# Products of probabilities and v for two query blocks in one session, one copy for both

## The chip, the cores and the metric

The kernel runs on one core of a Trainium2 chip. A core has TensorE (PE; its weight loads are listed as PEld), VectorE (DVE), ScalarE (ACT), GpSimd (POOL), SyncE (SP) and 16 DMA engines. The metric is the device time of one execution in microseconds. Lower is better.

## The reference

One transformer block over 2048 tokens of width 640. The condition `c` gives six modulation rows. The first half is sliding-window attention with 32 heads of 20 dimensions, in which a query sees itself and the 255 keys before it. The second half is an MLP of width 1536.

```python
mod = (_silu(c) @ w_mod).reshape(c.shape[0], 6, 1, -1)
h = _layernorm(x, axis=-1) * (1 + ca) + sa
# _A_ref: qkv = h @ wqkv; scores = q k^T * 20 ** -0.5
mask = (idx[:, None] - idx[None, :] >= 0) & (idx[:, None] - idx[None, :] < 256)
p = _softmax(jnp.where(mask, scores, -1e9), axis=-1)
x = x + ga * ((p @ v) @ wo)
h = _layernorm(x, axis=-1) * (1 + cb) + sb
x = x + gb * (_gelu(_layernorm(h) @ w1 + b1) @ w2 + b2)
```

## The kernel before, in words

Values that need more than one pass are split into a high and a low part, and each product is three matmuls (high x high, high x low, low x high). The program has four stretches: a prologue (first projections of q and k, modulation columns, the layer norm of the first tokens), the attention's loop, the passage to the second half, and the MLP. Every instruction goes through a helper that keeps the program's order on each engine, so the profile shows nearly all of them under line 193 (L193) and they are told apart by their tiles.

**The loop.** Its iterations are numbered `t`. The tokens are split into two halves of 1024 (`half`), the heads into 8 groups of four (`quad`), and a half into 8 query blocks of 128 (`qb`); 2 x 8 x 8 = 128 items. In iteration `t` there are, in this order:

- Scores `s` of item `t` (query by key), for the row maxima alone, and scores `e` of item `t - 11` (key by query; `LAG = 11`), for the exponentials. `score_batch` issues both as one batch of matmuls of 60 or 62 rows.
- `e_mask`: DVE masks `e`.
- `pv_stage`: a session of products of probabilities `pt` and `vbuf` (or `vcar`, the two key blocks carried from the first half). It runs in columns of 32, four heads beside each other, into PSUM tile `o`. A query block needs up to three key blocks, so a session has 4, 8 or 12 matmuls, which the profile shows as 8, 16 or 24 instructions, since each runs in two passes.
- `pv_copy`: ScalarE copies `o` to half of the tile `oT`. In the iterations of `SUMS_LAST` this stands behind the exponentials, otherwise ahead of them.
- `e_exp`: ScalarE takes the exponential of `e` into `pt` (five buffers, `NPT`), and GpSimd cuts the two triangles by two selections.
- `s_max`: DVE masks `s` and takes the maxima `nm`, in two pieces, or in one in the iterations of `WHOLE`.
- Four quarters `h` = 0 to 3, with whatever a plan has put there: at 0 and 2 the projection products (`pp`) of later heads, at 1 small turns that go through the `o` bank (`take_aside`), elsewhere loads, splits and casts, and from iteration 115 on the first work of the second half (`wo`, `xt`, `yt`).
- `pv_store`: a DMA from ScalarE's queue stores `oT`, once per two query blocks.

A query block's session stands in iteration `LAG + PVLAG + 8 * (8 * half + quad) + qb + half`, with `PVLAG = 2`: two iterations after the newest `pt` it reads was made.

**The planner.** `lay_units` spreads the 810 products of 54 projection units over the iterations up to `LAST = 108`. It finds by bisection a `room` per iteration, subtracts what turns cost, and adds the corrections of `EXTRA`. `UNITS` is the units' order, `EARLY` says when weights are split, `AFTER` delays turns. `LOV` lists units whose low parts DVE makes (GpSimd the rest), `HIA` casts that ScalarE makes. `MODS`, `WOS`, `W1S`, `RS`, `LNS`, `LATE_AT`, `TAIL0`, `NEXT`, `TAIL_AT`, `SHIFTS` and `MOVE` are times and engines of other pieces. `prepare` splits the MLP's weights in 18 pieces: ScalarE casts the high part, the engine of `PREPE` ("p" GpSimd, "d" DVE) subtracts for the low part, at the times of `PREP`. `WARM` puts idle matmuls into the loop, `ORDER` is the prologue's order.

Of the kernel before, what the change touches and what calls it, by code (L numbers as in the profile page):

```python
# [17 lines left out]
P = 128  # L18
# [9 lines left out]
VW = 21  # L28
# [4 lines left out]
PVLAG = 2  # L33
# [4 lines left out]
ORDER = 'T00 S0 L00 M1 R5 S1 R7 S2 T01 R3 S3 L01 N R6 P00 R6 M2 R2 T02 M3 P01 T03 L02 T10 R1 L10 L03 R5 C P02 T11 M4 T04 P10 T13 T12 L04 L12 L11 L13 P03 P04 E0 T14 L14 P11 Y00 P12 P13 Y01 P14'  # L38
LOWP = ['L00', 'L03', 'L10', 'L12', 'L04', 'L14', 'L02', 'L13']


UNITS = ((0, 'q1', 'k1', 'v0', 'v1', 'k2', 'q2', 'v2', 'q3', 'k3', 'v30', 'k40', 'q40', 'v40', 'q41', 'k41', 'v31', 'v41'), (1, 'q10', 'k00', 'q00', 'k10', 'q01', 'k01', 'k11', 'q11', 'v0', 'v1', 'k2', 'q2', 'k3', 'q3', 'v2', 'q4', 'v3', 'k4', 'v4'))
FAST = 10
LNS = [-10.75, -3.75, -1.0, -1.5, 1.75, -0.5, -0.25]
LOV = [1, 8, 15, 17, 18, 24, 25, 28, 31, 35, 37, 43, 44, 47, 52, 54, 55, 57]
HIA = [2, 5, 7, 9]
# [22 lines left out]
WOS = [86.25, 92.25, 98.25, 108.5, 111.75, 113.25, 118.0]
W1S = [126.25, 123.5]  # L70
RS = [[79.75, 80.25], [82.25, 84.25]]
# [4 lines left out]
NEXT = [133.869, 138.782]  # L76
# [3 lines left out]
TAIL_AT = {'rd': -1.3068, 'ri': -0.9678, 'load': -0.9467, 'om': -0.2491, 'oh': 0.0039, 'ol': 0.1278, 'w00': 0.2982, 'w01': 0.3513, 'w02': 0.405, 'w03': 0.4739, 'w04': 0.5616, 'add0': 0.569, 'sa0': 0.8046, 'w10': 0.711, 'w11': 0.7249, 'w12': 0.7775, 'w13': 0.7979, 'w14': 0.8778, 'add1': 0.885, 'sa1': 1.1777, 'm0': 1.3428, 'x0': 1.368, 'x1': 1.5837, 'm1': 1.344, 'sb0': 1.5278, 'sb1': 1.5966, 'n2': 1.7395, 'y0': 1.8473, 'y0l': 1.9709, 'y1': 2.026, 'y1l': 2.1439, 'xs': 1.5892}  # L80
# [9 lines left out]
PREPO = ['a0', 'a1', 'a2', 'a3', 'a4', 'a5', 'b0', 'b1', 'b2', 'b3', 'b4', 'b5', 'b6', 'b7', 'b8', 'b9', 'b10', 'b11']  # L90
PREP = [8.5, 14.5, 16.0, 24.0, 26.75, 29.0, 38.0, 39.75, 42.75, 49.75, 52.0, 53.75, 63.5, 66.25, 67.25, 74.5, 77.75, 79.75]
PREPS = [0.75, 1.25, 1.75, 1.25, 1.5, 0.5, 1.25, 1.75, 2.0, 1.0, 2.0, 2.5, 1.5, 2.5, 1.25, 1.25, 2.5, 1.75]
PREPE = 'pppppppddpppppppdp'
SHIFTS = {'xs.3': 0.0692, 'sb1.3': 0.0208, 'n2.3': 0.082, 'y0.3': 0.0208, 'y0l.3': 0.1499, 'y1.3': 0.229, 'y1l.3': 0.1312, 'y1.1': 0.0411, 'add0.3': 0.0437, 'sb0.4': -0.2255, 'n2.4': -0.3097, 'rd.1': -0.0806, 'w13.3': 0.0057, 'm1.4': -0.0777, 'x0.4': -0.0148, 'sb1.4': -0.2131, 'x1.4': -0.0788, 'w03.0': -0.0911, 'w13.0': 0.0783, 'xs.0': 0.0616, 'sa0.3': -0.1054, 'y1l.2': -0.0153, 'add1.3': 0.0891, 'x0.3': -0.1271, 'x1.0': -0.0318, 'sb1.0': -0.0318, 'rd.4': 0.0708, 'w04.0': -0.1766, 'add0.0': -0.1766, 'oh.2': -0.1264, 'ol.2': -0.1264, 'sa0.4': 0.1411, 'load.0': 0.0158, 'm0.3': -0.1391, 'x0.2': -0.0056, 'sb0.2': -0.0056, 'w13.1': -0.0028, 'sb0.3': -0.0998, 'x1.3': -0.0998, 'oh.3': 0.0453, 'ol.3': 0.0453, 'y1l.1': -0.0306, 'w10.2': -0.0083, 'w11.2': -0.0083, 'w12.2': -0.0083, 'ri.4': 0.0976, 'w10.3': -0.0663, 'ol.0': -0.0707, 'xs.2': 0.0752, 'w10.4': 0.0088, 'w10.0': -0.0992, 'sa0.1': -0.0354, 'w14.1': -0.0354, 'add1.1': 0.1001, 'y0l.1': 0.0457, 'sa1.1': -0.0249, 'w10.1': -0.0656, 'sa0.0': 0.0999, 'y0.4': -0.1354, 'xs.4': -0.1354, 'y0l.4': -0.1354, 'y1.4': -0.1354, 'y1l.4': -0.1354, 'n2.1': -0.0627, 'n2.2': 0.0408, 'y0.2': 0.0408, 'y0l.2': 0.0408, 'y1.2': 0.0408, 'x1.2': -0.0924, 'm0.0': -0.0138, 'w00.1': 0.0058, 'w01.1': 0.0058, 'w02.1': 0.0058, 'rd.3': -0.1006, 'w03.4': -0.0047, 'w02.0': -0.0393}
ROWS = [0, 1, 0, 0, 2, 0, 0, 0, 6, 0, 1, 5, 2, 0, 0, 1]
AHEAD = 5.25
# [102 lines left out]
def block_kernel(ctx: ExitStack, tc: tile.TileContext, x, wqkv, wo, w1, b1, w2, b2, c, crow, wmod, wcol, sel, outT):  # L199
# [1667 lines left out]
```

## Time and profile before

| | us |
|---|---|
| median of three runs | 961.62 (961.39 to 962.18) |
| profiled execution | 960.75 |
| its span | 959.0 |

| engine | busy, us | share of the span |
|---|---|---|
| PE | 932.4 | 97% |
| PEld | 739.9 | 77% |
| DVE | 657.8 | 69% |
| POOL | 498.7 | 52% |
| ACT | 412.0 | 43% |

The attention's loop fills about 50 to 580 us of the span; sessions run from 106.5 to 578.8. A timeline row gives start, length, engine, line, operation, output and inputs, the shape and how many instructions were merged into it; what stands in brackets is idle time ahead of it and what ended it. PE's lengths overlap, since its instructions are pipelined; distances between starts are what counts. "PEclk" is the clock granted to TensorE, as a share of full speed.

### The profile page before, as it was taken

How to read it: one execution, taken by the hardware profiler on the slowest of the kernel's cores; microseconds unless marked ns; L12 is line 12 of the kernel's file. 1: busy time of each engine (PE TensorE's matmuls, PEld its weight loads, DVE VectorE, ACT ScalarE, POOL GpSimd, SP SyncE). 2: the span in 40 equal slices, each digit the busy share in tenths (PEclk: the TensorE clock that was granted, in tenths of full speed). 3: DMA queues.
4: the chain of work that ended last, by engine and by line, in shares of the span. 5: the costliest groups of instructions: out<-in, count | busy, mean ns of one | idle time of the engine just before them, and what ended most of it. 6: DMA issues, size and time to landing. Idle time of an engine off the chain costs nothing.

```text
span 959.0 us, 20088 instructions
## 1 busy us (share of the span) xinstructions
PE 932.4 (97%) x7685; PEld 739.9 (77%) x7685; DVE 657.8 (69%) x1104; ACT 412.0 (43%) x729; POOL 498.7 (52%) x671
## 2 busy tenths in 40 slices
PE   9999999999999999999998899999999999999998
PEld 8867677776777777777676678888888888888886
DVE  5564878889768787766879977795557667633332
ACT  3633555576755565555544553441221324311111
POOL 3533656787966555375455556886242655311020
PEclk8999999999999999999989999999999999999999
DMA  8356989879799877945763439564649957644285
GB/s 311 99 191 184 343 260 327 279 214 303 243 310 282 275 228 253 289 144 144 222 183 103 127 99 337 152 223 143 241 166 332 300 178 242 214 167 177 104 278 188
DMA packets 109183, 212.34 MB, mean 221 GB/s; under 512 B 9856, under 2 KB 43104, under 8 KB 107552
## 3 DMA queue, kind: packets, MB, share of 16 engines
q1 hardware_dynamic: 99872, 202.67, 65.1%
q10 hardware_dynamic: 9216, 8.39, 2.8%
q8 instruction: 61, 1.00, 0.4%
q14 instruction: 34, 0.28, 0.1%
HBM read 137.44 MB, written 72.81 MB: 219 GB/s over the span
## 4 chain that ended last, share of the span: by engine, by line
PE 81%; DVE 10%; ACT 3%; DMA 2%; issue 2%; SPq 1%; POOL 0%; DVEq 0%; ACTq 0%; POOLq 0%
PE pp L193 17%; PE out L193 16%; PE P L193 15%; PE o L193 7%; PE e L193 7%; PE wo L193 6%; PE s L193 4%; DVE nm L193 2%; ACT pt L193 2%; DVE e L193 2%; PE ppo L193 2%; DVE s L193 1%; PE warm L193 1%; PE psx L193 1%; DMA wc<-in_wcol 1%
## 5 line engine op out<-in xcount | busy, mean ns | idle before, releaser
L193 POOL TENSOR_SCALAR_AFFINE_SELECT pt<-pt 128x512 f32<-128x512 f32 x192 | 131.8, 687 | 127.6 <-ACT pt L193 120.6
L193 PE MATMUL out<-ghi,w 128*128 128x512 f32 x480 | 168.3, 395 | 0.0
L193 ACT ACTIVATE pt<-e 128x1024 f32<-128x1024 f32 (+1 forms) x120 | 133.7, 1115 | 64.0 <-DVE e L193 61.1
L193 DVE TENSOR_REDUCE nm<-s 128x1 f32<-128x256 f32 (+4 forms) x194 | 156.7, 836 | 4.4
L193 PE MATMUL e<-qbuf,kbuf 62*128 62x128 f32 (+2 forms) x773 | 113.4, 330 | 13.2 <-ACT pt L193 11.7
L193 PEld LDWEIGHTS e<-qbuf,kbuf 62*128 62x128 f32 x773 | 80.8, 186 | 52.9 <-ACT pt L193 30.2
L193 PE MATMUL pp<-hhi,w_hi 128*128 128x512 f32 x265 | 114.8, 433 | 0.3
L193 PE MATMUL s<-kbuf,qbuf 60*128 60x384 f32 (+2 forms) x728 | 107.2, 305 | 3.4 <-DVE stage L193 1.4
L193 PE MATMUL pp<-hlo,w_hi 128*128 128x512 f32 x265 | 108.1, 408 | 0.0
L193 DVE COPY_PREDICATED e<-mask_t,e 128x512 f32<-128x512 uint32 x96 | 66.5, 693 | 58.3 <-PE e L193 51.4
L193 PE MATMUL pp<-hhi,w_lo 128*128 128x512 f32 x265 | 105.8, 399 | 0.0
L193 PEld LDWEIGHTS out<-ghi,w 128*128 128x128 f32 x480 | 90.1, 188 | 17.4 <-issue 0.7
L193 PE MATMUL o<-pt,vbuf 128*32 128x128 f32 x2688 | 100.6, 279 | 0.0
L193 PEld LDWEIGHTS s<-kbuf,qbuf 60*128 60x128 f32 x728 | 88.0, 187 | 13.9 <-DVE nm L193 5.5
L193 PE MATMUL out<-glo,w 128*128 128x512 f32 x240 | 93.9, 391 | 0.0
L193 POOL TENSOR_TENSOR w_lo<-wraw,w_hi 128x128 fp32r<-128x128 f32 x171 | 76.3, 478 | 23.7 <-ACT w_hi L193 21.9
L193 PE MATMUL P<-yhi,w1s 128*128 128x512 f32 x264 | 88.2, 389 | 0.0
L193 DVE COPY_PREDICATED s<-mask_t,s 128x512 f32<-128x512 uint32 x112 | 77.1, 688 | 14.7 <-PE s L193 14.7
L193 ACT COPY oT<-o 128x128 f32<-128x128 f32 x128 | 33.8, 264 | 119.0 <-PE o L193 116.8
L193 PEld LDWEIGHTS o<-pt,vbuf 128*32 128x32 f32 x2688 | 67.5, 110 | 15.3 <-issue 2.5
L193 PEld LDWEIGHTS pp<-hhi,w_hi 128*128 128x128 f32 x265 | 49.8, 188 | 22.1 <-issue 10.0
L193 PE MATMUL wo<-wo_h,ot_hi 128*128 128x320 f32 x256 | 60.9, 321 | 0.1
(230 smaller groups left out, 1782.0 us busy)
## 6 DMA issues: line engine op xcount, KB each, us to landing
w<-w_scr SPq DMA_DIRECT2D x48, 640.0 KB
qbuf<-q_scr SPq DMA_DIRECT2D x60, 240.0 KB
wraw<-in_wqkv SPq DMA_DIRECT2D x36, 320.0 KB
w_scr<-prep SPq DMA_DIRECT2D x18, 640.0 KB
kbuf<-k_scr SPq DMA_DIRECT2D x44, 240.0 KB
q_scr<-stage SPq DMA_DIRECT2D x20, 512.0 KB
k_scr<-stage SPq DMA_DIRECT2D x20, 512.0 KB
ws_scr<-w1s SPq DMA_DIRECT2D x6, 1536.0 KB
```

The source lines that it names most:

```text
L193: return self.tc.keep_in_program_order(op(*args, **kw))
```

## The change

A session makes two query blocks (`b` for blocks 2b and 2b + 1) one after the other, into the two halves of one `o` tile of 128 x 256, and one ScalarE copy empties it. There are 64 sessions in place of 128, with the same matmuls in all. A pair's session stands one iteration after its newest `pt` was made (`PVLAG = 1`); of the four pairs of a quad they fall on the item numbers 1, 3, 5 and 6 (+ `half`), plus `LAG + 1`. `pv_at` is made ahead of the planner, which charges each such iteration `PV_COST` products. A new table `SPOT` moves some sessions, with their copy, from behind the batch to a quarter of the iteration. The loop's tables are new.

```diff
-PVLAG = 2
+PVLAG = 1
-WARM = {(114, 3): 2, (135, 0): 1}
-LATE_AT = [105.25, 106.5, 107.25, 108.5, 110.75, 111, 113.5]
+WARM = {}
+LATE_AT = [105.75, 106.0, 106.75, 108.5, 109.75, 110.75, 114.25]
-PREP = [8.5, 14.5, 16.0, 24.0, 26.75, 29.0, 38.0, 39.75, 42.75, 49.75, 52.0, 53.75, 63.5, 66.25, 67.25, 74.5, 77.75, 79.75]
-PREPE = 'pppppppddpppppppdp'
+PREP = [7.5, 14.0, 15.0, 22.5, 25.5, 27.0, 36.75, 38.75, 41.75, 48.75, 50.0, 54.75, 63.5, 66.5, 67.5, 74.0, 79.0, 80.5]
+PREPE = 'ppppdpddpdddddddpd'
+PV_COST = 1.9833
+SPOT = {99: 3, 40: 3, 44: 3, 128: 2, 115: 1, 118: 1, 69: 1, 54: 1, 119: 3, 107: 3, 11: 3, 45: 3, 51: 3, 14: 2, 123: 3, 111: 3, 89: 3, 76: 3, 29: 1, 12: 3, 134: 3, 77: 2, 68: 2, 36: 3, 116: 1, 136: 1, 129: 3, 55: 2, 103: 2, 91: 2, 100: 3, 135: 2, 97: 3, 81: 1, 60: 1, 59: 1, 38: 1, 84: 3, 80: 3, 32: 2, 126: 1, 20: 1}
...
-    def pv_stage(half, quad, qb):
+    def pv_stage(half, quad, b):
         q = quads[half, quad]
-        ob = pools["o"].tile([P, P], F32, tag="o", name=f"o{half}_{quad}_{qb}")
...
+        ob = pools["o"].tile([P, 2, P], F32, tag="o", name=f"o{half}_{quad}_{b}")
+        for c in range(2):
+            qb = 2 * b + c
+            kbs = [kb for kb in range(qb - 2, qb + 1) if (kb, qb) in q["p"]]
+            for kb in kbs:
+                v = vblk(half, quad, kb)
+                pt, col = q["p"][kb, qb]
+                for i, h in enumerate(HEADS):
+                    matmul(
+                        ob[32 * h : 32 * h + 32, c], v[:, h * VW : h * VW + 32], pt[:, i, col : col + P],
+                        start=kb == kbs[0], stop=kb == kbs[-1], tile_position=(0, 32 * h), skip_group_check=True,
+                    )
...
-        nc.scalar.copy(q["oT"][:, c], ob)
+        q["oT"] = att.tile([P, 2, P], F32, tag="oT", bufs=2, name=f"oT{half}_{quad}_{b}")
+        nc.scalar.copy(q["oT"], ob)
...
+                u = min(2 * b + 1, 6) + half
+                pv_at.setdefault(LAG + PVLAG + (half * QUADS + quad) * NQB + u, []).append((half, quad, b))
...
+        for t in pv_at:
+            used[t] += PV_COST
...
-        sums = [(*key, pv_stage(*key)) for key in pv_at.get(t, ())]
+        sums = [] if t in SPOT else [(*key, pv_stage(*key)) for key in pv_at.get(t, ())]
...
+            if SPOT.get(t) == h:
+                for key in pv_at.get(t, ()):
+                    pv_copy(*key, pv_stage(*key))
```

Also new, with other numbers in the same form: `ORDER` (35 warming matmuls in both), `LOWP`, `UNITS`, `LNS`, `LOV`, `HIA`, `EXTRA`, `EARLY`, `AFTER`, `SUMS_LAST`, `WHOLE` (51 iterations of the main part before, 36 now), `MODS`, `WOS`, `W1S`, `RS`, `NEXT`, `TAIL_AT`, seven entries of `MOVE`, `PREPS`, `SHIFTS`, `ROWS` and `AHEAD`.

More of the change, by code (lines that the diff above doesn't have):

```diff
@@ new lines @@
+AFTER = {0: 2, 2: 3, 4: 4, 5: 2, 6: 1, 7: 1, 8: 2, 9: 1, 10: 2, 11: 2, 12: 1, 14: 2, 15: 1, 19: 1, 20: 1, 21: 2, 22: 1, 23: 2, 27: 1, 32: 1, 34: 1, 35: 1, 36: 2, 38: 3, 39: 6, 40: 2, 41: 1, 47: 4, 48: 1, 45: 4, 42: 2, 51: 3, 59: 1, 60: 2, 17: 2, 18: 1, 54: 1, 46: 1, 43: 1, 44: 1}
+SUMS_LAST = [15, 19, 26, 29, 33, 35, 42, 43, 50, 63, 65, 71, 74, 76, 79, 83, 86, 87, 88, 89, 90, 92, 93, 103, 104, 105, 106, 107, 108, 110, 111, 113, 114, 116, 117, 118, 119, 120, 121, 126, 130, 131, 133, 135, 136, 139, 140]
@@ L70 @@
-W1S = [126.25, 123.5]
-RS = [[79.75, 80.25], [82.25, 84.25]]
+MODS = [[7.25, 16.0], [18.0, 27.0], [68.75, 80.0], [54.75, 65.0]]
+WOS = [90.25, 93.5, 101.25, 109.25, 113.25, 114.25, 117.0]
+W1S = [124.5, 122.75]
+RS = [[79.5, 80.75], [88.75, 91.0]]
 TOMID = 109
-WARM = {(114, 3): 2, (135, 0): 1}
-LATE_AT = [105.25, 106.5, 107.25, 108.5, 110.75, 111, 113.5]
+WARM = {}
+LATE_AT = [105.75, 106.0, 106.75, 108.5, 109.75, 110.75, 114.25]
 TAIL0 = [115.25, 120.25, 124.25, 129.25]
-NEXT = [133.869, 138.782]
+NEXT = [133.869, 138.574]
@@ L97 @@
+ROWS = [2, 1, 0, 0, 4, 0, 0, 0, 2, 0, 0, 5, 4, 0, 0, 4]
+AHEAD = 4.75
 W2B = 3
@@ L774, in e_exp, with pv_copy, pv_store @@
             )
-    def pv_stage(half, quad, qb):
+    def pv_stage(half, quad, b):
         q = quads[half, quad]
-        ob = pools["o"].tile([P, P], F32, tag="o", name=f"o{half}_{quad}_{qb}")
-        kbs = [kb for kb in range(qb - 2, qb + 1) if (kb, qb) in q["p"]]
-        for kb in kbs:
-            v = vblk(half, quad, kb)
-            pt, col = q["p"][kb, qb]
-            for i, h in enumerate(HEADS):
-                matmul(
-                    ob[32 * h : 32 * h + 32], v[:, h * VW : h * VW + 32], pt[:, i, col : col + P],
-                    start=kb == kbs[0], stop=kb == kbs[-1], tile_position=(0, 32 * h), skip_group_check=True,
-                )
+        ob = pools["o"].tile([P, 2, P], F32, tag="o", name=f"o{half}_{quad}_{b}")
[10 more added lines that the diff above has]
+                    )
         return ob
-    def pv_copy(half, quad, qb, ob):
+    def pv_copy(half, quad, b, ob):
         q = quads[half, quad]
-        b, c = divmod(qb, 2)
-        if c == 0:
-            q["oT"] = att.tile([P, 2, P], F32, tag="oT", bufs=2, name=f"oT{half}_{quad}_{b}")
-        nc.scalar.copy(q["oT"][:, c], ob)
-        if qb == NQB - 1:
-            done_v.add(half * QUADS + quad)
-    def pv_store(half, quad, qb):
-        b, c = divmod(qb, 2)
-        if c:
-            t0 = half * HALF + b * 256
-            nc.scalar.dma_start(o_scr[quad * 4 : quad * 4 + 4, :, t0 : t0 + 256], quads[half, quad]["oT"].rearrange("p c t -> p (c t)"))
+        q["oT"] = att.tile([P, 2, P], F32, tag="oT", bufs=2, name=f"oT{half}_{quad}_{b}")
+        nc.scalar.copy(q["oT"], ob)
+        if b == NQB // 2 - 1:
+            done_v.add(half * QUADS + quad)
+    def pv_store(half, quad, b):
+        t0 = half * HALF + b * 256
+        nc.scalar.dma_start(o_scr[quad * 4 : quad * 4 + 4, :, t0 : t0 + 256], quads[half, quad]["oT"].rearrange("p c t -> p (c t)"))
     box2 = {}
@@ L1332, in take_aside @@
         return t
+    pv_at = {}
+    for half in range(2):
+        for quad in range(QUADS):
+            for b in range(NQB // 2):
+                u = min(2 * b + 1, 6) + half
+                pv_at.setdefault(LAG + PVLAG + (half * QUADS + quad) * NQB + u, []).append((half, quad, b))
     def lay_units(room):
@@ L1502, in block_kernel @@
     n = len(s_items)
-    pv_at = {}
-    for half in range(2):
-        for quad in range(QUADS):
-            for qb in range(NQB):
-                pv_at.setdefault(LAG + PVLAG + (half * QUADS + quad) * NQB + qb + half, []).append((half, quad, qb))
-    for t in range(n + LAG + PVLAG + 4):
+    for t in range(n + LAG + 6):
         now[0] = t
```

32 lines of the change are left out of this document (13 added, 19 removed).

## The prediction

> **What bounds the kernel now.** I read the page first: the engines' totals.
>
> ```profile
> PE 932.4 (97%) x7685; PEld 739.9 (77%) x7685; DVE 657.8 (69%) x1104; ACT 412.0 (43%) x729; POOL 498.7 (52%) x671
> ```
>
> TensorE is busy 97% of 959.0 us. Next the stages, with the products of probabilities and v (tile `o`) by themselves; columns are length, then busy time and count for PE, PEld, DVE, ACT and POOL (the second answer has PE, PEld and ACT alone), granted clock, DMA share and GB/s.
>
> ```profile
> 98.70:466.00 367.30, 361.75 (x3997) 268.20 (x3997) 292.51 (x410) 212.10 (x395) 236.00 (x355) 1.00 0.81 256
> 466.00:500.00 34.00, 31.87 (x390) 24.23 (x390) 26.35 (x34) 18.48 (x35) 19.49 (x22) 0.90 0.73 205
> 500.00:580.00 80.00, 70.28 (x980) 55.08 (x978) 68.31 (x117) 38.62 (x67) 42.87 (x60) 1.00 0.43 128
> ```
>
> ```profile
> 98.70:466.00 367.30, 75.85 (x2064) 50.63 (x2064) 24.87 (x94) 1.00 0.81 256
> 466.00:580.00 114.00, 30.40 (x816) 20.83 (x816) 8.93 (x34) 0.97 0.52 151
> ```
>
> In the main part of the attention loop (iterations 13 to 107) PE idles 367.30 - 361.75 = 5.55 us: there PE time is the time. In the tail it idles 2.13 + 9.72 us, and DVE is busy 68.31 of 80, so PE time saved there is worth less. ScalarE copies `o` once per session: 94 sessions in the main part, 34 in the tail, 128 in all. The change makes 64.
>
> **What a session costs.** Time order on PE: an iteration without a session (345.28), and two with one of 24 instructions (348.64, 352.68).
>
> ```profile
> 345.28 0.56 PE L193 MATMUL e<-qbuf,kbuf 62*128 62x256 f32 x3
> ...
> 346.36 0.49 PE L193 MATMUL pp<-hhi,w_hi 128*128 128x512 f32 x1
> 346.69 0.39 PE L193 MATMUL pp<-hlo,w_hi 128*128 128x512 f32 x1
> 346.92 0.40 PE L193 MATMUL pp<-hhi,w_lo 128*128 128x512 f32 x1
> ...
> 348.64 0.56 PE L193 MATMUL e<-qbuf,kbuf 62*128 62x256 f32 x3
> ...
> 349.75 0.65 PE L193 MATMUL o<-pt,vcar 128*32 128x128 f32 x16
> 350.21 0.40 PE L193 MATMUL o<-pt,vbuf 128*32 128x128 f32 x8
> 350.54 0.50 PE L193 MATMUL pp<-hhi,w_hi 128*128 128x512 f32 x1
> ...
> 352.68 0.56 PE L193 MATMUL e<-qbuf,kbuf 62*128 62x256 f32 x3
> ...
> 354.50 0.50 PE L193 MATMUL pp<-hhi,w_hi 128*128 128x512 f32 x1
> ```
>
> ```profile
> 106.55 0.42 PE L193 MATMUL o<-pt,vbuf 128*32 128x128 f32 x8
> 106.91 0.50 PE L193 MATMUL pp<-hhi,w_hi 128*128 128x512 f32 x1
> ```
>
> From the score batch to the first projection product it takes 1.08 us without a session, 1.90 and 1.82 with one: 0.82 and 0.74 more. A session of 8 takes 0.36 to the next product, one of 24 takes 0.79 (349.75 to 350.54); 16 more instructions cost 0.43, so 24 stream in 0.645. The rest, 0.10 to 0.18, is paid for being a session of its own; I take **0.15**, nearer to the middle.
>
> In the table SPOT, 15 of the 64 sessions leave the place behind the score batch (the other keys meet no session): 8 in the main part, of which 4 stand at the end of their iteration, just ahead of the next batch, and 4 in the midst of products; 7 in the tail, 5 of them in the midst. A session amid full-array products occurs late in the trace:
>
> ```profile
> 574.00 0.31 PE L193 MATMUL wo<-wo_h,ot_lo 128*128 128x320 f32 x1
> 574.24 0.86 PE L193 MATMUL o<-pt,vbuf 128*32 128x128 f32 x24
> 575.03 0.56 PE L193 MATMUL wo<-wo_h,ot_hi 128*128 128x320 f32 x2
> 575.42 0.31 PE L193 MATMUL wo<-wo_h,ot_lo 128*128 128x320 f32 x1
> 575.57 0.46 PE L193 MATMUL wo<-wo_h,ot_hi 128*128 128x320 f32 x2
> ```
>
> A product of `wo` streams in 0.15 (575.42 to 575.57). So its own part is 0.24 - 0.15 ahead, 0.79 - 0.645 in it, 0.39 - 0.30 behind: 0.33, which is 0.18 more than behind the batch. A session at the iteration's end the trace doesn't show: between 0 and 0.18 more; it also has one batch as neighbour, so I take 0.
>
> Main part: 94 - 48 = 46 sessions less, 46 x 0.15 = 6.9; moved ones cost 4 x 0.18 = 0.7; **gain 6.2** (46 x 0.10 - 8 x 0.18 = 3.2 to 46 x 0.18 = 8.3). Tail: 34 - 16 = 18 less, 2.7, minus 5 x 0.18 = 0.9: 1.8 of PE time, at most that; with PE not the bound there I count **0.3** (from 0).
>
> The Trainium skill (TensorEngine Tiling (Array Packing), Key Properties) says that a change of tiling mode drains TensorE, a change of tile doesn't. By that rule only changes of mode count: 46 - 4 = 42 fewer in the main part, an estimate of 42 x 0.09 = 3.8 us with the 0.09 of the row at 574.24, and the time would come out 2.4 us above mine, inside the forecast's own band below, so it has no chance of its own. The rows of whole sessions decide for me.
>
> **What the longer sessions have to wait for.** PVLAG goes from 2 to 1: the newest `pt` of a pair was made one iteration earlier, not two. Its making, then the pieces that move:
>
> ```profile
> L193 DVE COPY_PREDICATED e<-mask_t,e 128x512 f32<-128x512 uint32 x96 | 66.5, 693 | 58.3 <-PE e L193 51.4 <-PE s L193 3.1 <-ACT y L193 1.8
> L193 DVE TENSOR_REDUCE nm<-s 128x3 f32<-128x768 f32 x63 | 60.4, 959 | 2.1
> L193 DVE TENSOR_REDUCE nm<-s 128x4 f32<-128x1024 f32 x49 | 60.1, 1226 | 1.7
> L193 DVE TENSOR_REDUCE nm<-s 128x1 f32<-128x256 f32 x63 | 26.0, 413 | 0.0
> L193 DVE TENSOR_TENSOR prep<-prep 128x640 fp32r<-128x640 f32 x3 | 3.0, 1016 | 0.0
> ...
> L193 ACT ACTIVATE pt<-e 128x1024 f32<-128x1024 f32 x96 | 98.8, 1030 | 41.5 <-DVE e L193 41.2
> ...
> L193 POOL TENSOR_SCALAR_AFFINE_SELECT pt<-pt 128x512 f32<-128x512 f32 x192 | 131.8, 687 | 127.6 <-ACT pt L193 120.6
> ```
>
> Mask, exponential and two selections: 0.69 + 1.03 + 2 x 0.69 = 3.10 us. The iteration at 345.28, without a session and with nine products (0.23 each, 346.69 to 346.92), lasts 3.36. Counted through the planner's rule with the new tables, iterations without a session get 8.3 products on average and those with one 5.1: 3.36 - 0.7 x 0.23 = 3.20 us. The newest `pt` is read only by the last 8 of 48 instructions, 40 x 0.645 / 24 = 1.08 after the session's start. So the undisturbed chain has some 3.20 + 1.08 - 3.10 = 1.2 us to spare. It isn't always undisturbed:
>
> ```profile
> 297.51 2.12 POOL L193 TENSOR_TENSOR w_lo<-wraw,w_hi 128x128 fp32r<-128x128 f32 x5
> 299.60 1.27 POOL L193 TENSOR_TENSOR stage<-pf,stage 128x512 fp32r<-128x512 f32 x1
> 300.84 2.15 POOL L193 TENSOR_TENSOR prep<-prep 128x640 fp32r<-128x640 f32 x1
> 302.94 1.34 POOL L193 TENSOR_SCALAR_AFFINE_SELECT pt<-pt 128x512 f32<-128x512 f32 x2
> ```
>
> ```profile
> 300.61 0.86 PE L193 MATMUL o<-pt,vbuf 128*32 128x128 f32 x24
> ```
>
> These three POOL pieces put the selections off to 304.28 (302.94 + 1.34); a pair in place of the session at 300.61 would have read that `pt` at 301.69 and waited 2.6 us, with all of PE's queue behind it. With lag 2 nothing waits. The new PREPE takes 8 of 15 `prep` subtractions from POOL; of those left, two (times 14.0 and 22.5) lie in the iteration ahead of a session. Bounds: 0, and 2 x 2.6 = 5.2. I take **1.0**.
>
> **DVE.** It gains 8 x 1.02 = 8.1 us from `prep`, and 15 maxima cut in two (WHOLE falls from 51 to 36) at 0.959 + 0.413 - 1.226 = 0.15 each, 2.2. So 292.51 + 10.3 over 95 iterations: 3.19 us each, against the 3.20 of an iteration without a session; iterations with a session leave it room. I take **0.4** lost (0, to 0.5 in each of the some 8 short iterations of 4 or 5 products: 4).
>
> **At nothing.** ScalarE copies 64 times twice as much; its 24.87 us in the main part at most stay, hidden under 367.30 - 212.10 of idle, and exponentials that queue behind the longer session have the next batch's start as their date. DMA stores of `oT` stay at 64. ORDER keeps 35 warming products, and the prologue's other moves, like MOVE, TAIL_AT and SHIFTS, I hold at 0 (-1 to +1): they put pieces on engines that stand beside PE. AFTER, EXTRA, EARLY and UNITS shift work within an unchanged count of iterations (LAST stays 108).
>
> **Sum.** 6.2 + 0.3 - 1.0 - 0.4 = 5.1 us less. The profiled execution took 960.75 (span 959.0, 1.75 around it), so 955.6; the runs' median is 0.87 above that execution: **956.5**.
>
> **Rivals.** (a) *The newest `pt` comes late, and it gets slower.* PE stands at the last third of a pair for POOL. At 2.6 us a time it decides from (6.5 - 0.4) / 2.6, some 2.4 sessions (3 to be slower by 0.2%); with four of 48, 961.6 - 6.1 + 10.4 = 966. For it: POOL is busy 236.0 of 367.30 and its order is fixed. Against it: the 8 pieces gone, and waits on `pt` are short so far:
>
> ```profile
> PE e L193 <- ACT pt L193: 2.1, 6, 0.9
> ```
>
> (those are from 98 to 450 us). (b) *DVE takes the gain.* Score banks aren't doubled, so where iterations without a session are DVE's, PE waits at the next batch: 0.1 in each of 47, with the 1.0 of (a), gives back 5.7: 961. For it: 3.19 against 3.20. Against: the mean hides that session iterations are longer. (c) *No half-clock stage.* The clock fell after a gap that the profile shows:
>
> ```profile
> 487.00:490.40 3.40, 2.06 (x37) 1.55 (x36) 2.79 (x3) 2.73 (x4) 3.18 (x5) 1.00 0.43 130
> 490.40:493.80 3.40, 3.03 (x42) 2.43 (x43) 2.47 (x4) 0.87 (x2) 1.25 (x1) 0.72 0.38 115
> 493.80:497.20 3.40, 3.16 (x31) 2.49 (x33) 2.63 (x4) 1.36 (x4) 0.00 (x0) 0.50 0.85 243
> 497.20:500.60 3.40, 3.40 (x46) 2.68 (x42) 1.84 (x3) 1.19 (x2) 1.27 (x2) 0.77 0.94 226
> ```
>
> That lost 3.4 x (0.28 + 0.50 + 0.23) = 3.4 us. A session in the midst of iteration 115 and a last unit that reaches to 114.25 fill just this stretch: 953. Against it: tail iterations without a session will have PE idle over a third of their time elsewhere. The Trainium skill (TensorE: Matmul & The Clock Gate, HAM oscillation — how this bites in real kernels) has the gate close on idle gaps over about 3.4 us; by that rule none should close here. The trace disagrees: 2.06 us of busy time in 3.40 was enough. (d) *A second such stage*, for the same reason and since WARM is emptied: 956.5 + 3.4 = 960.
>
> **How the numbers follow.** A measurement tells 0.2%, 1.9 us, from no change: faster is below 959.7, slower above 963.5. Chances: forecast (953.5 to 959.5 with its terms' likely errors) 0.39, (a) 0.13, (b) 0.17, (c) 0.22, (d) 0.09. Faster: the forecast's, (c)'s and half of (d)'s, 0.66; slower: (a)'s and a little of (b), 0.14; the rest, 0.20, is the same. The range, 951 to 963.5, reaches 2 below (c), whose gain term has that much room, and takes in (b) and (d); (a) is left out above.
>
> **What will show it.** Right: 64 copies of `oT` of 256 elements; sessions of 48 taking some 1.44 us to the next product; batch to product 1.08 without a session; PE busy in the loop less by about 8 us. Wrong: PE idle at `o` for POOL or ACT `pt` (a), at `s` or `e` for DVE over 6 us in the main part (b). Clock rows of 0.5 settle (c) and (d).

## The result and the profile after

The changed kernel is slower by half a per cent: median 966.18 us (964.31 to 968.84, four runs) against 961.90 for the kernel before, ratio 1.0053 (95% interval 1.0036 to 1.0071). Run again beside other kernels later, it took 965.81 against 960.31, ratio 1.0059 (1.0025 to 1.0094). The forecast was 956.5, and the range up to 963.5 doesn't hold it.

The profiled execution took 964.31 us, its span 962.6. The engines' totals of the page:

```profile
PE 926.6 (96%) x7679; PEld 741.6 (77%) x7679; DVE 665.8 (69%) x1125; ACT 410.8 (43%) x672; POOL 483.9 (50%) x659
```

TensorE is busy 5.8 us less than before, and the span is 3.6 us longer: it stands still more. Where, the stretches tell. The bounds are the starts of the score batches of iterations 13 and 108, and of the MLP's first product `P`; the last bound is the start of the last `out` product. First the kernel before, then the changed one (columns as in the prediction: length, busy time and count of PE, PEld, DVE, ACT and POOL, clock, DMA share, GB/s):

```profile
105.53:466.02 360.49, 355.11 (x3956) 263.14 (x3955) 287.52 (x403) 207.59 (x389) 232.34 (x350) 1.00 0.81 254
466.02:579.41 113.39, 101.54 (x1363) 78.80 (x1362) 94.11 (x150) 57.10 (x102) 62.36 (x81) 0.97 0.52 150
579.41:954.40 374.99, 374.77 (x1820) 315.71 (x1819) 216.92 (x405) 98.86 (x154) 159.86 (x169) 1.00 0.63 214
```

```profile
103.62:462.03 358.41, 351.90 (x4006) 267.37 (x4005) 291.65 (x419) 204.51 (x344) 224.30 (x343) 1.00 0.81 254
462.03:580.82 118.79, 100.30 (x1312) 78.89 (x1308) 93.59 (x153) 58.27 (x89) 60.35 (x80) 0.97 0.52 149
580.82:958.27 377.45, 375.69 (x1820) 315.46 (x1818) 218.85 (x405) 98.89 (x154) 159.99 (x169) 1.00 0.62 211
```

| stretch | before | after | difference |
|---|---|---|---|
| to iteration 13 | 105.53 | 103.62 | -1.9 |
| iterations 13 to 107 (main part) | 360.49 | 358.41 | -2.1 |
| iteration 108 to the MLP (tail) | 113.39 | 118.79 | +5.4 |
| MLP's products | 374.99 | 377.45 | +2.5 |
| behind them (span's end) | 4.6 | 4.3 | -0.3 |

Of the 4.0 us gained up to iteration 108, the first 1.9 are not the change's. The clock stood at a half for 6.8 us ahead of iteration 13 in this execution of the kernel before and for 3.4 us in that of the changed one. The first 50 us, before and after:

```profile
0.00:50.00 50.00, 46.36 (x284) 42.50 (x284) 27.90 (x107) 26.62 (x39) 22.30 (x34) 0.93 0.59 197
```

```profile
0.00:50.00 50.00, 45.75 (x293) 41.22 (x294) 31.61 (x116) 26.60 (x39) 17.01 (x30) 0.97 0.61 207
```

Over the 20 profiled executions of this study, the start of iteration 13 goes by that: 102.7 and 103.0 us where the clock did not fall ahead of it, 103.0 to 103.8 with 3.4 us at a half, 105.1 to 105.5 with 6.8. Each of the last two groups has kernels with the prologue of before and with the new one. So the change gains the main part's 2.1 us, and the tail gives back more than twice that.

The sessions themselves came out as forecast. In the changed kernel's time order on PE there is a pair of 48 instructions (290.05), and two iterations without a session (284.83, 292.39):

```profile
284.83 0.56 PE L195 MATMUL e<-qbuf,kbuf 62*128 62x256 f32 x3
...
286.08 0.50 PE L195 MATMUL pp<-hhi,w_hi 128*128 128x512 f32 x1 [0.16 <-ACT pf L195]
...
290.05 1.52 PE L195 MATMUL o<-pt,vbuf 128*32 128x128 f32 x48
291.49 0.50 PE L195 MATMUL pp<-hhi,w_hi 128*128 128x512 f32 x1
...
292.39 0.56 PE L195 MATMUL e<-qbuf,kbuf 62*128 62x256 f32 x3
...
294.36 0.50 PE L195 MATMUL pp<-hhi,w_hi 128*128 128x512 f32 x1 [0.79 <-ACT pf L195]
```

A pair takes 1.44 us to the next product, two sessions of 24 took 2 x 0.79: 0.14 saved a pair. But batch to first product takes 1.25 and 1.97 in these two iterations without a session, not 1.08: the product stands for ScalarE's second copy (`pf`) out of the projection bank. Of the 45 such iterations of the main part whose batch has twelve instructions, 26 take 1.01 to 1.11, as forecast, and 19 take 1.18 to 1.97. PE's waits in the main part (98 to 462 us; in all, times, longest) have it:

```profile
PE pp L195 <- ACT pf L195: 1.9, 8, 0.8
```

The same view of the kernel before has no such row: a session stood between batch and products in nearly every iteration, and it covered that copy.

PE's waits in the tail (466 to 582 us), before and after:

```profile
PE e L193 <- ACT pt L193: 8.3, 13, 1.8
PE wo L193 <- POOL ot_lo L193: 0.8, 1, 0.8
```

```profile
PE e L195 <- ACT pt L195: 8.4, 12, 1.5
PE wo L195 <- POOL ot_lo L195: 2.8, 3, 1.4
PE e L195 <- DMA qbuf<-mlo: 2.1, 1, 2.1
```

New are 2.1 us for the DMA of `mlo` and 2.0 more for `ot_lo`.

### The profile page after: what moved, and what is told of

Its sections match the earlier page's. It is cut to its first block, busy times and chain, and to the rows that moved or that the text cites. A ratio compares the mean times of both kernels' runs of the same rounds, so it can differ in the third digit from the quotient of the medians.

```text
span 962.6 us, 19953 instructions
## 1 busy us (share of the span) xinstructions
PE 926.6 (96%) x7679; PEld 741.6 (77%) x7679; DVE 665.8 (69%) x1125; ACT 410.8 (43%) x672; POOL 483.9 (50%) x659
## 4 chain that ended last, share of the span: by engine, by line
PE 79%; DVE 6%; ACT 5%; DMA 4%; POOL 3%; issue 2%; SPq 1%; ACTq 0%; DVEq 0%; POOLq 0%
PE pp L195 18%; PE out L195 15%; PE P L195 13%; PE o L195 8%; PE e L195 7%; PE wo L195 6%; PE s L195 4%; ACT pt L195 2%; PE ppo L195 2%; DVE e L195 2%; PE warm L195 1%; DVE nm L195 1%; PE xt L195 1%; PE psx L195 1%; DMA wc<-in_wcol 1%
## 5 line engine op out<-in xcount | busy, mean ns | idle before, releaser
L195 POOL TENSOR_SCALAR_AFFINE_SELECT pt<-pt 128x512 f32<-128x512 f32 x192 | 133.9, 697 | 122.9 <-ACT pt L195 116.1
L195 DVE TENSOR_REDUCE nm<-s 128x3 f32<-128x768 f32 (+4 forms) x209 | 157.7, 787 | 4.4
L195 PE MATMUL o<-pt,vbuf 128*32 128x128 f32 x2688 | 89.7, 277 | 0.2 <-ACT pt L195 0.2
L195 PEld LDWEIGHTS o<-pt,vbuf 128*32 128x32 f32 x2688 | 71.1, 111 | 10.8 <-issue 3.7
L195 PEld LDWEIGHTS pp<-hhi,w_lo 128*128 128x128 f32 x265 | 50.0, 189 | 13.4 <-issue 1.4
```

The costliest lines, as they stand in the source:

```text
L195: return self.tc.keep_in_program_order(op(*args, **kw))
```

## The experiments

Ratios are against the kernel before on the same chip, with 95% intervals. The theories were three: (A) the main part's gain is lost at the projection bank, where the session no longer covers ScalarE's copy; (B) iterations without a session last as long as VectorE's chain of two masks and maxima; (C) tail and MLP lose because of their new tables. Their rivals stand in the expectations.

### The copy ahead of the products

In the unit's copies of q and k, where ScalarE makes them, the full value comes first and the high part is cast from it, so that the bank is free one copy earlier. In the changed kernel (after_pf) and in the one before (before_pf).

```diff
+            if eng is not nc.vector:
+                nc.scalar.copy(box["st"][:, 0], box["f"])
+                return
             nc.scalar.mul(box["st"][:, 0], box["ps"], sc)
...
-        ev = [v_copy, v_turn(0, 4)] if kind == 2 else [qk_hi, qk_full, qk_lo]
+        ev = [v_copy, v_turn(0, 4)] if kind == 2 else [qk_hi, qk_full, qk_lo] if eng is nc.vector else [qk_full, qk_hi, qk_lo]
```

> The changed kernel; where GpSimd makes the low part of a projection, ScalarE reads the product's PSUM bank once (full value first) and makes the high part from that copy in SBUF, so the bank is free one 0.6 us copy earlier. Theory A (lost cover: without a session between batch and products, the first product of a unit waits for ScalarE's second copy): the 16 waits of the first product behind a batch, 4.3 us together in the main part, fall under 1 us, and the time falls by about 3 us, to 963. Rival B (the gain went to other waits that pace the iterations, DVE above all): the waits move elsewhere, time within 1 us of the changed kernel.

> The kernel before with the same order of ScalarE's two copies. Theory A: its sessions cover these copies already, so nothing is gained: within 1 us of 961.9. If the bank's release is a price that both kernels pay, it gains 2 us or more.

Measured: 967.62 us, ratio 1.0054 (1.0025 to 1.0084), and 959.97, ratio 0.9990 (0.9972 to 1.0008). In after_pf the wait is all but gone, yet the main part, 358.01 us, is 0.4 us shorter, no more:

```profile
PE pp L195 <- ACT pf L195: 0.3, 1, 0.3
```

By the starts of the score batches, iteration 27 shrinks from 3.27 to 3.06 us and iteration 28 grows from 3.42 to 3.63; 38 and 39, 60 and 61, 84 and 85 do the same. In iteration 28 it is the batch that takes longer, 1.27 us to its first product in place of 1.07, after a start that is 0.44 us earlier. In seven other executions with the same sessions up to iteration 107, and tables that differ at most in its last three iterations, the main part took 358.2 to 359.8 us, so 0.4 is no measurable gain, and theory A's 963 did not come. The wait of theory A is real, though no view has the 16 waits of 4.3 us together that I expected (PE's row has 8 of 1.9), and it stood beside others of about its length.

### Sessions and tables apart

pairs_old has sessions in pairs with every table of before (SPOT empty, PV_COST 0), single_new the kernel before's single sessions at lag 2 with all the new tables (ORDER to AHEAD).

```diff
-PV_COST = 1.9833
+PV_COST = 0.0
+SPOT = {}
```

> The changed kernel's sessions in pairs with every table of the kernel before, no session moved to a quarter, no charge for a session in the planner. If the pairing gains by itself and the new tables lose it, this is below 961.9 (956 to 960). If the newest pt comes late for pairs unless GpSimd is relieved, sessions show waits on pt of 3 us or more in the main part and the time is 965 to 972.

> The kernel before, one query block a session and lag 2, with the new tables. If the new tables cost the end of the loop (5 us lost from iteration 128 to the MLP, 2.5 in the MLP) whatever the sessions, that loss shows here too and the time is 968 or more. If the loss there belongs to the pairs, the end of the loop is as in the kernel before and the time about 962.

Measured: 993.89 us, ratio 1.0329 (1.0298 to 1.0359), and 989.42, ratio 1.0283 (1.0261 to 1.0304). Main part 385.21 and 379.12 us. Neither half works with the other's tables, and no forecast came near. In pairs_old PE waits (98 to 488 us) show the mechanism of rival (a):

```profile
PE o L195 <- POOL pt L195: 5.8, 5, 2.6
```

Five sessions stand up to 2.6 us for GpSimd's `pt`; that is 5.8 of the some 25 us by which the main part is longer. The same view of the changed kernel has no such row: its tables avert the wait. Which of them does was not tried. Since tables and sessions fit each other, these two runs say little on either alone.

### Is it VectorE?

One more VectorE piece in iterations 13 to 107, a maximum over 128x256 of a constant, read by nothing: behind the maxima of the scores (dve), or ahead of them, between mask and maxima (chain, shown).

```diff
+        if 13 <= now[0] < 108:
+            nc.vector.tensor_reduce(more, mask_t[:, 0:2], AX.X, ALU.max)
         del maxima[:]
```

> The changed kernel with one more VectorE piece in each of iterations 13 to 107, a maximum over 128x256 of a constant that nothing reads, behind the maxima of the scores; by the row of the 128x256 maxima some 0.41 us each, 39 us in all. Theory B (iterations without a session last as long as VectorE's chain of mask, mask and maxima, and so give the sessions' gain back): each of the 47 without a session grows by nearly the whole piece: the main part is 10 to 19 us longer, and clearly more so than in the kernel before with the same piece. Theory A (only the wait for the projection bank gives it back; VectorE has room): under 5 us, and about as much as in the kernel before.

> The kernel before with the same VectorE piece in iterations 13 to 107. VectorE would be busy 292.5 + 39 of 367 us, 3.49 a iteration against a mean period of 3.79. Theory B: a session in every iteration leaves the piece room, the main part grows by 0 to 5 us. Theory A: as in the changed kernel with the piece, within 3 us.

> The changed kernel with the constant's maximum (0.41 us) not behind the maxima of the scores but ahead of them, between the mask of s and its maxima, in iterations 13 to 107. There it lies in the chain from a batch through two masks and the maxima to the next batch's bank, which a piece behind the maxima doesn't lengthen. Theory B (this chain, not VectorE's total, limits iterations without a session): the main part grows by 10 to 18 us, against the 4.2 of the piece behind the maxima, and by at least 3 us more than the kernel before does with the same piece. Theory A (no such limit): 4 to 6 us, as behind the maxima.

> The kernel before with the same piece at the same place. Theory B: the session in every iteration covers much of it, the main part grows by 4 to 9 us and by at least 3 less than in the changed kernel. Theory A: by 3 to 5 us, as behind the maxima (3.5), and within 2 us of the changed kernel.

Main part: 362.65 us (after_dve, +4.2), 364.01 (before_dve, +3.5), 366.39 (after_chain, +8.0) and 368.71 (before_chain, +8.2).

```profile
103.68:470.07 366.39, 357.83 (x4004) 270.92 (x4003) 310.44 (x514) 204.47 (x344) 223.78 (x343) 1.00 0.79 248
```

```profile
102.73:471.44 368.71, 361.67 (x3956) 266.89 (x3955) 307.60 (x498) 207.90 (x389) 232.30 (x350) 1.00 0.78 248
```

The same piece costs both kernels the same within 0.7 us. VectorE, by its total or by the chain through masks and maxima, doesn't limit the changed kernel more than the one before: rival (b) and my theory B fall. Theory A's 4 to 6 us did not come either: between mask and maxima the piece costs twice what it costs behind them, so this chain does pace some iterations, in both kernels alike. (The whole times were 971.78, 967.96, 975.97 and 970.08 us; they hold an MLP that all four had longer, see below.)

### What loses the tail

after_tail_before gives the changed kernel the tail's tables of before. hybrid has, besides, single sessions from the thirteenth group of heads on. tail_pairs is the reverse: the kernel before with every table it had, and pairs from the thirteenth group on. The choice in hybrid's `pv_at`, with ONES = 12 (session, copy and store follow it):

```diff
+            if half * QUADS + quad >= ONES:
+                for qb in range(NQB):
+                    pv_at.setdefault(LAG + 2 + (half * QUADS + quad) * NQB + qb + half, []).append((half, quad, qb))
+                continue
             for b in range(NQB // 2):
```

> The changed kernel with the end of the loop as it was before: tables WARM, LATE_AT, NEXT, TAIL_AT, MOVE and SHIFTS whole, ROWS from its fourteenth entry, SUMS_LAST and WHOLE from iteration 108, and no session moved from 108 on. The sessions stay in pairs. Theory C (the new tables lose the MLP's 2.5 us and most of the tail's 4.9): the MLP takes 375 us from its first product, as before, not 377.4; iterations 128 to 138 some 30 to 31 us, not 33.8; time 959 to 961. Rival (longer sessions themselves loosen the tail, and the clock falls wherever TensorE idles): the MLP back to 375, but 128 to 138 stays at 33 or more, time 962 to 964. If the MLP stays at 377.4 these tables are not its cause.

> As the run with the end of the loop as before, and the last four groups of heads (from iteration 109 on) have a session for each query block, with lag 2 and a copy each, as before; the first twelve groups in pairs. Theory C with the pairs good for the main part alone: prologue and main part as in the changed kernel (4 us less than before between them, less some 1 us of products that go back into the tail), tail and MLP as before: 957.5 to 959, faster than before by some 3 us. Rival (pairs are no loss in the tail): the same time as the run with pairs throughout, within 1 us. If the main part's gain was only work pushed into the tail: 961 to 962, as before.

> The kernel before with all its tables, and pairs of query blocks (lag 1, one copy each) from the thirteenth group of heads on alone, that is from iteration 108 on; until there single sessions. If pairs themselves lose time where TensorE isn't the bound (iterations without a session last 2.8 us or more for the chain of masks and exponentials, those with one get longer): iterations 108 to the MLP 117 to 119 us, not 113.4, the MLP 375 as before, time 965 to 967. If the new tables are what loses it: 113 to 114 us and 960.5 to 962.

Measured: 966.87 us, ratio 1.0055 (1.0039 to 1.0071); 962.52, ratio 1.0021 (1.0001 to 1.0041); 967.94, ratio 1.0066 (1.0042 to 1.0090). So the tables of before don't mend the tail (119.12 us in after_tail_before), against my theory C, and the pairs alone break it: main part and tail of tail_pairs,

```profile
105.38:465.92 360.54, 355.09 (x3956) 263.13 (x3955) 287.60 (x403) 207.69 (x389) 232.34 (x350) 1.00 0.82 254
465.92:585.52 119.60, 101.84 (x1362) 80.68 (x1362) 94.53 (x150) 55.99 (x86) 62.60 (x81) 0.97 0.50 145
```

which is 6.2 us more in the tail with the same mean clock and nothing else touched. By the starts of the batches 4.2 of them lie in iterations 108 to 127 and 0.4 in 128 to 137. The other 1.6 lie between the last batch and the MLP, where the last pair stands 0.96 us for ScalarE's newest `pt`, the price of lag 1. How the first part comes about, PE's time order tells, for the same two iterations before and in tail_pairs:

```profile
502.63 0.56 PE L193 MATMUL e<-qbuf,kbuf 62*128 62x256 f32 x3
...
503.71 0.64 PE L193 MATMUL o<-pt,vcar 128*32 128x128 f32 x16
...
506.02 0.56 PE L193 MATMUL e<-qbuf,kbuf 62*128 62x256 f32 x3
...
507.34 0.62 PE L193 MATMUL o<-pt,vbuf 128*32 128x128 f32 x16
...
509.27 0.56 PE L193 MATMUL e<-qbuf,kbuf 62*128 62x256 f32 x3 [0.24 <-ACT pt L193]
```

```profile
502.81 0.56 PE L194 MATMUL e<-qbuf,kbuf 62*128 62x256 f32 x3 [0.30 <-ACT pt L194]
...
504.32 0.65 PE L194 MATMUL o<-pt,vcar 128*32 128x128 f32 x16
...
505.22 0.62 PE L194 MATMUL o<-pt,vbuf 128*32 128x128 f32 x16
...
507.28 0.55 PE L194 MATMUL e<-qbuf,kbuf 62*128 62x256 f32 x3
...
509.14 0.31 PE L194 MATMUL wo<-wo_hi,ot_lo 128*128 128x320 f32 x1
510.11 0.56 PE L194 MATMUL e<-qbuf,kbuf 62*128 62x256 f32 x3 [0.66 <-ACT pt L194]
```

Two iterations with a session each take 6.64 us (502.63 to 509.27). With a pair in the first and none in the second they take 4.47 + 2.83 = 7.30. The second has too little work: PE is done at 509.45 and stands 0.66 us for ScalarE's exponential, which has to empty the bank of `e`. The batch itself (some 1.1), mask (0.69) and exponential (1.03), one behind the other, set a floor of 2.83 us (the iterations 116, 119 and 124 of tail_pairs take just that). So the iteration that loses its session is only 0.42 us shorter, and the one with the pair is 1.08 longer: 0.65 for the second session, and 0.43 since its batch, behind a wait of its own, takes 1.51 us to the session (502.81 to 504.32) in place of 1.08. In the main part the planner's PV_COST puts more products into the iteration without a session. The tail's work stands at fixed times, and no product is left to put there.

In the changed kernel these tail iterations (117, 119) take 3.00 and 2.83 us, those with pairs (118, 120) 4.09 and 3.86. With single sessions hybrid's tail takes 116.62 us, still 3.2 more than before, but 2.85 of that lie in iterations 114 and 115, where a load comes late (next step) and the clock falls; the rest of its tail is that of the kernel before within 0.4.

### SyncE's queue

hybrid still waits 3.1 us in iteration 114: the maxima's low part, made at 480.8, is loaded at 484.73, since the loads of `r` and `xb` stand ahead of it in SyncE's queue, and `r` goes out only at 482.82. (What holds `r`, the trace doesn't settle.)

```profile
482.82 0.56 SPq L196 DMA_DIRECT2D r<-r_scr  x1
483.47 0.55 SPq L196 DMA_DIRECT2D xb<-in_x  x1
484.11 0.57 SPq L196 DMA_DIRECT2D qbuf<-mhi  x1
484.73 0.54 SPq L196 DMA_DIRECT2D qbuf<-mlo  x1
...
488.42 0.87 PE L196 MATMUL e<-qbuf,kbuf 62*128 62x128 f32 x5 [3.05 <-DMA qbuf<-mlo]
```

In the kernel before, at the same times, that cost nothing: its PE came to iteration 114 3.7 us later (486.4, not 482.7). hybrid_rows and after_mlo put the two loads behind the maxima's.

```diff
+            if nm == "load" and bg == 0:
+                tail.append((112.25, nm, lambda gos=gos: [go() for go in gos[1:]]))
+                gos = gos[:1]
```

> The run in pairs to group twelve and single sessions behind it, with one edit more: the loads of the row sums r and of the block of x for the first block of the second half stand behind the loads of the maxima (mhi, mlo) in SyncE's queue, at 112.25, not ahead of them. There they wait for a store and hold the maxima back, for which TensorE waited 3.1 us in iteration 114. If that order is the cause: no wait on mlo, iterations 114 and 115 take 8.3 us as before, not 11.1, and without that pause the clock falls in less time there; time 957 to 959.5, 2 to 4 us under the kernel before. Rival (the maxima are late for another reason): the wait stays, time as without the edit, 961 to 963.

> The changed kernel with the same edit alone: the loads of r and x behind those of the maxima. If the order in SyncE's queue is the cause of the 2.1 us wait in iteration 114, that iteration falls from 5.5 to some 3.4 us. If the tail passes it on, iterations 108 to 128 take 74.5, not 76.5 us, and the time is 964; if another wait behind it takes it up, 76.5 and 966.

Measured: 961.02 us, ratio 0.9996 (0.9981 to 1.0012), and 965.08, ratio 1.0041 (1.0024 to 1.0058). The order was the cause: no wait on `mlo` is left in either, and iteration 114 takes 4.1 us in hybrid_rows and 4.4 in after_mlo. In after_mlo the tail falls from 118.79 to 117.31 us, with 6.8 us of half clock in both; in the whole time the two can't be told apart. hybrid_rows still missed its forecast of 957 to 959.5. In its profiled execution, the slowest of its twelve runs, the clock stood at a half for 10.2 us from 489 and 6.8 from 551.

### Idle windows and the clock

The clock changes on a grid of 3.41 us. PE's windows just ahead of a change, in the kernel before (488.49, the clock falls; 546.52, it does not), before_pf, the changed kernel and hybrid (it falls behind each):

```profile
488.49:491.90 3.41, 2.07 (x31) 1.74 (x35) 2.48 (x4) 1.72 (x2) 3.01 (x3) 1.00 0.10 29
546.52:549.93 3.41, 2.20 (x37) 1.44 (x36) 2.79 (x5) 2.01 (x4) 1.41 (x3) 1.00 0.47 143
```

```profile
544.41:547.82 3.41, 1.84 (x34) 1.33 (x34) 3.16 (x7) 2.01 (x4) 1.52 (x3) 1.00 0.53 159
```

```profile
535.18:538.59 3.41, 1.64 (x14) 1.20 (x12) 3.38 (x6) 1.18 (x2) 0.87 (x2) 1.00 0.06 20
```

```profile
484.05:487.46 3.41, 1.32 (x28) 0.93 (x20) 2.94 (x3) 2.33 (x3) 1.39 (x2) 1.00 0.58 173
```

Counted over the 20 profiled executions of this study from iteration 13 on: 37 windows had a fall behind them, all with PE busy 0.67 of the window or less; some 4800 at full clock had none, all with 0.54 or more, and 46 of these with no more than 0.67. So between 0.54 and 0.67 the share alone doesn't decide. The three kernels of this step fill such windows with idle matmuls: hybrid_warm (on hybrid_rows) and before_warm by the first table, after_warm by the second (between 116 and 127 in the `o` bank).

```diff
+WARM = {(114, 3): 5, (130, 3): 4, (135, 0): 1}
+WARM = {(114, 3): 4, (115, 3): 3, (120, 3): 1, (121, 0): 3, (125, 0): 2, (127, 3): 3, (129, 3): 3, (130, 3): 2, (132, 3): 1, (135, 3): 3}
```

> Pairs to group twelve, single sessions behind it, r and x loaded behind the maxima, and idle matmuls where TensorE otherwise stands still for over 1 us: WARM is 5 in the last quarter of iteration 114, 4 in that of 130, and 1 at 135 as before. In the traces so far the clock falls to a half for 3.4 us or more behind a window of 3.41 us in which TensorE was busy less than some 0.6, and this kernel has three such places from 480 us on. Clock theory: no half-clock stage in the loop's end or just one at 135; 957 to 958, faster than before by 3 to 4 us, and the runs lie closer together (all within 3 us, not 7.8). If idle windows are not what the clock follows: stages as in the run without the idle matmuls, 961.

> The kernel before with the same idle matmuls (WARM 5 at 114, 4 at 130, 1 at 135), nothing else. Clock theory: the stage of 6.8 us at 492 goes, 958 to 959.5, some 2 us under the kernel before. If idle windows are not what the clock follows: the stage stays, 961.

> The changed kernel with idle matmuls at the ten places of iterations 114 to 135 where its trace shows TensorE still for 0.5 to 2 us. Clock theory: no half-clock stage from 480 us on, iterations 108 to the MLP some 114 to 115 us and not 118.8, time 961 to 962.5: as the kernel before, that is the unused half of the loss is the clock's; what then remains is the MLP's 2.5 us and waits in the tail. If the stages are not from idle windows: 966 as without them.

Measured: **hybrid_warm 958.11 us (956.31 to 959.22, twelve runs), ratio 0.9967 (0.9953 to 0.9981)**; before_warm 960.17, ratio 0.9993 (0.9974 to 1.0012); after_warm 963.97, ratio 1.0045 (1.0028 to 1.0061). hybrid_warm beats both kernels, the one before by 0.3%. Its tail, the shortest of all, with the clock at full:

```profile
463.40:576.02 112.62, 100.14 (x1332) 77.70 (x1328) 93.89 (x151) 57.14 (x101) 62.48 (x81) 1.00 0.52 152
```

before_warm shows no gain that can be measured; its profiled execution still had a stage of 3.4 us at 496, behind iteration 115, which the idle matmuls don't reach. So how much of hybrid_warm's 0.3% is the pairs' and how much the clock's stays open: without the idle matmuls (hybrid_rows) it is not there, and the kernel before with the window behind iteration 115 filled was not run. after_warm's tail is down to one stage (521) and still takes 118.63 us, though its idle matmuls lengthen iterations as well (114 from 5.52 to 6.25 us, 123 from 4.11 to 6.09). With tail_pairs, which has the 6.8 us of half clock of the kernel before, this says that the half clock is not the main part of what the pairs lose there.

### The same kernels again

> The changed kernel, unaltered, for a second profiled execution. If the change itself slows the MLP: 377.5 us from its first product again, within 0.3. If what slows it is how VectorE's and GpSimd's pieces and the weight loads happen to meet in one execution: another figure between 375 and 378.5. The iterations 108 to the MLP, at equal time in half-clock stages, repeat within 0.5 us in both cases; the stages themselves may stand elsewhere.

> The kernel before, unaltered, for a second profiled execution. If its MLP is steady: 375.0 us within 0.3. If it changes from one execution to the next: between 375 and 378.5. Iterations 13 to 107: 360.5 us within 0.2 in both cases.

Tail and MLP of the second profiled executions, the changed kernel first:

```profile
462.45:583.17 120.72, 103.11 (x1311) 81.18 (x1308) 93.67 (x153) 58.33 (x89) 59.63 (x80) 0.94 0.51 145
583.17:959.74 376.57, 375.50 (x1819) 315.70 (x1819) 217.55 (x405) 98.59 (x154) 159.80 (x169) 1.00 0.61 211
```

```profile
466.07:579.57 113.50, 101.63 (x1362) 78.86 (x1362) 94.07 (x150) 57.08 (x102) 62.24 (x81) 0.97 0.51 149
579.57:956.18 376.61, 375.33 (x1819) 315.81 (x1819) 217.88 (x405) 98.94 (x154) 159.87 (x169) 1.00 0.62 213
```

The MLP takes 376.6 us in both, 377.45 and 374.99 the first time: it changes from one execution to the next and is no loss of the change. The tail's loss repeats: 120.72 against 113.50 (of which more half clock is a part: 13.6 us of it against 6.8), as does the main part's gain, 2.2 us (358.67 against 360.85). The clock has a part in the medians too: its median was 0.991 in these three runs and 0.9955 in the ten of the kernel before beside them. Among the runs of the kernel before alone, 0.001 less goes with 0.3 to 0.6 us more. By that, an estimate, 1.4 to 2.8 of the 5.5 us between the two medians go with the clock.

## Why the prediction was wrong

- **A session's own cost, 0.15, and 6.2 us in the main part: size right, yield half.** Measured 0.14 a pair. The main part is 2.1 us shorter; with lag 1 it also holds two more query blocks (2112 `o` instructions, row below, not 2064; 48 at 0.645 / 24 is 1.3), so 3.4 of 6.2 came. PE's busy time from iteration 13 to the MLP fell by 4.5 us, not by about 8. The cost I hadn't named is the first product behind the batch, for which the vanished session had covered ScalarE's copy (1.9 us of PE's own waits in the main part, none before). after_pf shows that this cover alone isn't the 2.8 missing: waits of like length stand beside it.

```profile
103.62:462.03 358.41, 67.78 (x2112) 54.50 (x2112) 17.46 (x47) 1.00 0.81 254
```

- **Newest `pt`, 1.0, and rival (a): the mechanism is real, the tables avert it.** No such wait in the changed kernel's main part, 5.8 us in the five sessions of pairs_old. In the tail of tail_pairs the last pair did stand 0.96 us for its `pt`.
- **DVE, 0.4, and rival (b): no.** after_chain and before_chain lose alike, and PE's waits for VectorE's `nm` in the main part are 0.6 us in all. The 10.3 us more of VectorE were mis-sized: it is 4.1 (287.52 to 291.65). The eight `prep` pieces brought 8.7 and the maxima 1.7 (of the main part's iterations, `WHOLE` had 40 before and has 28 now, not 51 and 36), but other pieces became fewer or shorter.
- **"At nothing": the prologue, right.** The 1.9 us up to iteration 13 are the clock's; from iteration 0 to 13 it takes 55.5 us before and 55.1 now. So iteration 108 begins 4.0 us earlier, near the 4.8 that the steps together had, but by luck: the change brought 2.1 of them.
- **The tail, "with PE not the bound there I count 0.3 (from 0)": this step failed.** It lost 5.4 us. I took the sign from PE's idle time alone: what PE saves there is worth little, but never less than nothing. In truth the work became lumped: an iteration without a session has a floor of 2.83 us from batch, mask and exponential, and the one with the pair gets longer by the whole session and more. tail_pairs shows 6.2 us from this edit alone, 4.2 of them where this lumping was; hybrid, with single sessions, is back at the times of before but for two iterations. The prediction had the numbers: DVE busy 68.31 of 80 and waits for ScalarE's `pt`, on which it remarked only that PE time is worth less.
- **Rivals (c) and (d).** In the first profiled execution the stage at 492 is gone and two others came (539, 566), 6.8 us of half clock as before: no net cost there. In the second there are four (490, 514, 541, 568), 13.6 us. So (c) did not come, its empty stretch was luck of the grid, and (d) had a part: the same unevenness opens other idle windows.
- **The MLP at 0: right,** though the first profile alone seemed to say +2.5.

What stays open: which waits take the rest of the main part's 2.8 us, how the gain would share out in a tail planned for pairs, and what the kernel before would gain from a clock kept up as in hybrid_warm.

## What to carry to other kernels

Merging small jobs saves their switches only where the freed time can be filled: an iteration that loses its job keeps the floor of its slowest chain, and the iteration that gets two grows by the whole of it. So merge where a planner can move work into the gap, keep single jobs where the work is fixed, and look at each stretch by itself, since here a gain of 2 us and a loss of 5 stood side by side, and a clock stage elsewhere looked like a gain. When an engine gets ahead, look at what stands in order in the DMA queues and at what the removed job used to cover.

## What the runs showed of the hardware

- **The clock follows PE's busy share in windows of a free-running grid.** The same kernel fell at different places in different executions (23, 539 and 566 us; 15, 490, 514, 541 and 568), since the grid starts elsewhere each time: the window at 546.52 above, busy 2.20 of 3.41, passed, and 2 us earlier on before_pf's grid 1.84 did not. The Trainium skill (TensorE: Matmul & The Clock Gate, Part 1: The HAM clock gate) gives a free-running window of 3413 ns and a fall after an idle one; the trace agrees with the grid, while a busy share of 0.39 to 0.61 was little enough in the rows above, with no gap longer than 2.1 us in the loop of the changed kernel's first trace. Filling two windows made hybrid_warm's runs lie within 2.9 us of each other; hybrid_rows' lay within 7.8.
- **A sum or difference on VectorE stands still while GpSimd works on a wide tile, if GpSimd began first.** Two executions of the kernel before differ by this in their MLP. In the first, VectorE's `glo` began 0.24 us ahead of GpSimd's `ra`; in the second 0.04 us behind it, and then it took 1.79 us in place of 0.69, and TensorE stood for it. There the second execution loses 1.2 of the 1.6 us by which its MLP is longer.

```profile
808.23 0.69 DVE L193 TENSOR_TENSOR glo<-gr,ghi 128x512 fp32r<-128x512 f32 x1
808.47 1.61 POOL L193 TENSOR_TENSOR ra<-ra,rb 128x512 f32<-128x512 f32 x1
```

```profile
808.94 1.28 POOL L193 TENSOR_TENSOR ra<-ra,rb 128x512 f32<-128x512 f32 x1
808.98 1.79 DVE L193 TENSOR_TENSOR glo<-gr,ghi 128x512 fp32r<-128x512 f32 x1 [0.36 <-ACT ghi L193]
810.83 0.50 PE L193 MATMUL out<-glo,w 128*128 128x512 f32 x1 [0.92 <-DVE glo L193]
```

VectorE's `wr` of 128x256 does the same in the first traces of before, hybrid and the changed kernel: it took 0.41 to 0.43 us where it began first, and ended 0.28 to 0.29 behind GpSimd's piece wherever one of 128x128 or wider had begun first, after up to 1.82 us. Beside GpSimd's `rsb` of 128x1, begun 0.65 us ahead, it was not slowed.

The Trainium skill (SBUF — State Buffer, Who interferes with whom) calls the port pair that the two share an exclusive lock, and has a VectorE instruction with two SBUF inputs contend with a GpSimd instruction that reads SBUF; the wide pieces agree, the case of `rsb` does not. How such meetings fall differs between executions, and with them the MLP's time.
- The four kernels with the added VectorE piece had an MLP of 378.7 to 380.5 us, with the same instructions as the others'. In before_dve it loses some 0.3 us in every 12 in two stretches (from 100 to 155 and from 250 us on, counted from its first product) and next to nothing elsewhere. They hold one constant tile of 8 bytes per partition more; whether that shift is the cause wasn't tried.
